# Loading q's and k's second pieces through SP in float32 instead of through GpSimd in bf16

## The chip, the core and the metric

The kernel runs on one core of one Trainium2 chip. The metric is the device time of one execution in microseconds. The times in this document come from repeated runs; the traces come from one profiled execution each, whose own time is given beside them. The engines are called TensorE, VectorE (DVE in the profile), ScalarE (ACT), GpSimd (POOL) and SyncE (SP). A load can be issued from SP, ScalarE or GpSimd; loads issued from GpSimd change float32 to bf16 on the way in this kernel, those from SP and ScalarE copy the bytes as they are.

## What is computed

Sliding-window attention with a linear distance bias over a batch of 8 with 8 heads, 576 positions and a head size of 64, followed by a two-layer block whose nonlinearity is h cos(h):

```python
scores = (q @ k.T) / sqrt(D)                    # per batch and head, float32 inputs
rel = pos[:, None] - pos[None, :]
scores = where((rel >= 0) & (rel < 128), scores - slopes[h] * abs(rel), -1e9)
attn = softmax(scores)
x = (attn @ v).transpose(0, 2, 1, 3).reshape(4608, 512)
h = x @ w_in                                    # 512 -> 2048
out = (h * cos(h)) @ w_out                      # 2048 -> 512, float32 output
```

## The kernel before

The work on TensorE is done in bf16. Attention runs in units: a unit is a batch, a block of 128 queries and (for blocks 1 to 3) half of the heads; a batch has eight units. For a unit, `scores` multiplies keys and queries into two PSUM banks, `exps` takes the exponential on ScalarE, `mask` multiplies by the bias and window factors on VectorE (the first units in `BIASED` instead get the bias added by a matmul on the same banks, in `scores`), `pv` multiplies by V, `norm` divides by the sum, and `x_pe` or `x_dma` transposes the result into `xT`. The two-layer block then takes 512 tokens at a time (`NCH` = 9 chunks): `moe1` makes 128 features of h and its cosine, `moe2` multiplies by W_out and stores. Chunk 0 is cut finer (`moe1_part`), so that it can begin with the first 128 tokens.

Queries and keys must stand with the head size on partitions. For batches 0 and 1 TensorE transposes them (`qk_transposes`), and VectorE or ScalarE copies the transposed bank to `tr`; for later batches DMA transposes do. Batch 0 comes in four pieces of tokens, so that its first unit can start early:

```python
PIECES = {0: [(0, 4, [(0, 4)]), (128, 4, [(0, 4)]), (256, 8, [(0, 4), (4, 8)]), (512, 2, [(0, 2)])], ...
```

Piece 0 covers tokens 0 to 127, piece 1 (the second) 128 to 255, piece 2 (the third) 256 to 511, piece 3 the last 64. Piece 0 is loaded by SP (q) and ScalarE (k) in float32 into `qF` and cast on VectorE or ScalarE to `qC`. The other pieces are loaded by GpSimd straight into bf16 (`qB`, `qE`). GpSimd's loads are issued in the order in which they are written: q's and k's second pieces, V's first block, q's and k's third pieces, V's second block, then W_in, more of V, the last pieces, q and k of batch 1, W_out and V of batch 1.

Every step is given to a planner (`Plan.op`) with what it reads and writes, the engine or the engines that may do it, how long it occupies the engine (`occ`), when its result is there (`lat`), and a priority (`pri`, low first). `Plan.schedule` runs through time with these figures and writes the order of each engine; among what can start at about the same time it takes the lowest priority, then what was created first. `emit` then writes the engines' programs in that order, with waits on semaphores. On the chip each engine follows its order and waits where the figures were wrong. For GpSimd's loads the planner keeps one `wire`:

```python
wire = max(wire, st + 2300) + o.lat              # starts at 4000
o.end = max(wire, st + o.occ + 1400) + 500
```

while a load on SP or ScalarE that is no transpose and no store ends at `st + o.lat`. In the first microseconds TensorE also runs matmuls on zeros (`filler`, line 944) where the plan has nothing else for it.

In the main program, the loads are created first (lines 878 to 893), then the transposes of the first two pieces (lines 895 to 897) and of k's third piece (line 898), which go to PSUM banks 0 and 1. Then `attention(every[0:7], -1)` (line 901) creates the first seven units, two at a time on banks 4, 5 and 6, 7; the transposes of q's third piece are created inside it after the second unit (line 843), on banks 6 and 7.

Of the kernel before, what the change touches and what calls it, by code (L numbers as in the profile page):

```python
# [7 lines left out]
ACTF = mybir.ActivationFunctionType  # L8
F32 = mybir.dt.float32
# [25 lines left out]
class Plan:  # L35
# [16 lines left out]
    def op(self, eng, fn, r=(), w=(), dma=None, occ=100, lat=None, pri=5, mode=0, table=None,  # L52
           after=()):
        o = Op()
        o.seq = len(self.all)
        o.eng = (eng,) if isinstance(eng, str) else tuple(eng)
        o.fn, o.r, o.w, o.dma = fn, tuple(r), tuple(w), dma
        o.occ, o.lat, o.pri, o.mode, o.table = occ, occ if lat is None else lat, pri, mode, table
        preds = {}
        for k in o.r:  # L60
            if k in self.writer:
                preds[self.writer[k]] = DATA
        for k in o.w:
            if k in self.writer:
                preds[self.writer[k]] = DATA
            for d in self.readers.get(k, ()):
                preds.setdefault(d, WAR)
        if dma is not None and dma in self.lastdma:
            preds[self.lastdma[dma]] = DATA
        for d in after:  # L70
            preds.setdefault(d, ORDER)
        if eng == "pool":
            if eng in self.lastseq:
                preds.setdefault(self.lastseq[eng], ORDER)
            self.lastseq[eng] = o
        if dma is not None:
            self.lastdma[dma] = o
        o.preds, o.succs, o.npred = preds, [], len(preds)
        for d in preds:
            d.succs.append(o)  # L80
        for k in o.r:
            self.readers.setdefault(k, []).append(o)
        for k in o.w:
            self.writer[k], self.readers[k] = o, []
        self.all.append(o)
        return o
# [200 lines left out]
def bass_alibi_sliding__then__act_gcu_kernel(  # L287
# [8 lines left out]
    with ExitStack() as ctx:  # L296
        def sb(name, shape, dt=BF16):
            return ctx.enter_context(nc.sbuf_tensor(name, shape, dt))

        R = Plan(nc, ctx)  # L300
        op = R.op
# [3 lines left out]
        xT = sb("xT", [128, NPAIR, NTOK])  # L305
        gT = [sb(f"gT{i}", [128, NFC, CH]) for i in range(2)]
        qF = {"q": sb("qfirst", [128, 2, 256], F32), "k": sb("kfirst", [128, 2, 256], F32)}
        qC = {"q": sb("qcast", [128, 4, 2, 64]), "k": sb("kcast", [128, 4, 2, 64])}
        qB = {"q": sb("qrows", [128, 2, 1152]), "k": sb("krows", [128, 2, 1152])}
        qE = {"q": sb("qend", [128, 2, 128]), "k": sb("kend", [128, 2, 128])}  # L310
# [51 lines left out]
        def piece_keys(which, b, n):  # L362
            return [("qB", which, i) for i in range(3)] if b else [("qB", which, n)]

        def load_qk(which, src, b, n=0):
            t0, rr, _ = PIECES[b][n]
            c0 = 64 * (t0 // 32)
            rows = bass.AP(src.tensor, src[b].offset + 64 * t0,
                           [[64 * rr, 32], [64 * S, H], [1, 64 * rr]])
            if b == 0 and n == 0:  # L370
                op("sp" if which == "q" else "act", [lambda e: e.dma_start(qF[which][:, :, :], rows)],
                   w=[("qF", which)], dma=f"ld{which}f", occ=700 if which == "q" else 2000,
                   lat=4000 if which == "q" else 3300, pri=0)
                i = qF[which][:, :, :].rearrange("p y (j d) -> p y j d", j=4)
                o = qC[which][:, :, :, :].rearrange("p j y d -> p y j d")
                op(("act", "dve"),
                   {"act": lambda e: e.activation(o, i, ACTF.Copy),
                    "dve": lambda e: e.tensor_copy(o, i)},
                   r=[("qF", which)], w=piece_keys(which, b, n), occ={"act": 460, "dve": 330},
                   lat={"act": 560, "dve": 410}, pri=2)  # L380
                return
            o = qE[which][:, :, :] if t0 == 512 else qB[which][:, :, c0:c0 + 64 * rr]
            op("pool", [lambda e: e.dma_start(o, rows)],  # L383
               w=piece_keys(which, b, n), dma=f"ld{which}{n}", occ=750,
               lat={2: 600, 4: 800 if which == 'q' else 900,
                    8: 2600 if which == 'q' else 1300, 18: 2850}[rr])

        def load_v(b, order=range(NBLK), behind=()):
            for t in order:
# [440 lines left out]
        def attention(us, phase):  # L830
# [45 lines left out]
            return begin  # L876

        load_qk("q", q, 0, 0)
        load_qk("k", k, 0, 0)
        constants()  # L880
        load_qk("q", q, 0, 1)
        load_qk("k", k, 0, 1)
        load_v(0, [0])
# [27 lines left out]
        for c in range(NCH):  # L911
# [17 lines left out]
            n = QUOTA[c] if c < len(QUOTA) else 0  # L929
# [46 lines left out]
```

## Time and profile before

| | |
|---|---|
| median of 3 runs | 310.22 us (309.71 to 310.29) |
| the profiled execution | 309.37 us, of which its span is 307.2 us |
| TensorE busy | 298.8 us (97%) |
| VectorE, ScalarE, GpSimd busy | 194.2, 200.0, 97.0 us |
| granted TensorE clock | 1.00 |
| DMA | 39.08 MB, mean 127 GB/s |

A line of the profile gives the engine, the line of the kernel, the operation, the output and the input by the program's names, and their shape. In a timeline a row starts with its start and its duration in us; the bracket at its end gives how long the engine had been idle before it and what released it. "PEld" is TensorE's weight load. A matmul's duration includes its way through the array, so the rows of matmuls that follow one another overlap. In the rows of DMA issues the last number is the time from the issue to the landing. In the windows, each row is a stretch of the span with its length, the busy time of TensorE, its weight loads, VectorE, ScalarE and GpSimd (with the number of instructions), the granted clock, the share of the DMA engines and their GB/s.

### The profile page before, as it was taken

The page shows a single profiled execution, that of the slowest core. Times are in us where ns is not written, and L with a number is a line of the kernel's source. Part 1 is how long each engine was busy: PE and PEld are TensorE (multiplying, and loading weights), DVE is VectorE, ACT ScalarE, POOL GpSimd, SP SyncE. Part 2 cuts the span into 40 slices and gives each one's busy share as a digit, 9 for nine tenths or more (in the row PEclk, how much of TensorE's full clock was granted, in tenths as well). Part 3 has the DMA queues.
Part 4 walks back from the last instruction along what each step waited for, and adds up shares of the span by engine and source line. Part 5 has one row for each costly group of instructions (what it writes and reads, how often), then busy time and mean ns, then how long its engine had stood idle before and what let it go on. Part 6 is the DMA issues. An engine that isn't in the chain of part 4 may idle for free.

```text
span 307.2 us, 6416 instructions
## 1 busy us (share of the span) xinstructions
PE 298.8 (97%) x2556; PEld 156.6 (51%) x2600; DVE 194.2 (63%) x407; ACT 200.0 (65%) x268; POOL 97.0 (32%) x122
## 2 busy tenths in 40 slices
PE   7899999999999999999999999999999999999996
PEld 5585455445544555445544554455445554444444
DVE  7687776674668566856785578657966588742000
ACT  7888855885498646883688378736964588752211
POOL 8997201364055505550357033900500000000000
PEclk9999999999999999999999999999999999999999
DMA  9999999999499939997699969995991420002112
GB/s 142 175 204 207 207 164 191 169 151 181 111 133 144 189 78 144 136 169 103 149 132 150 145 117 148 156 183 114 140 117 44 113 68 2 0 0 70 68 74 97
DMA packets 150332, 39.08 MB, mean 127 GB/s; under 512 B 138912, under 2 KB 145312, under 8 KB 150304
## 3 DMA queue, kind: packets, MB, share of 16 engines
q0 software_dynamic: 100688, 18.10, 79.9%
q1 hardware_dynamic: 49344, 20.33, 32.9%
q8 instruction: 20, 0.33, 0.5%
q10 hardware_dynamic: 272, 0.26, 0.3%
q14 instruction: 8, 0.07, 0.1%
HBM read 36.70 MB, written 9.44 MB: 150 GB/s over the span
## 4 chain that ended last, share of the span: by engine, by line
PE 83%; DMA 7%; POOL 5%; ACT 2%; issue 1%; DVE 1%; POOLq 0%; ACTq 0%
PE ps L812 37%; PE ps L759 36%; DMA w_outb<-in_moe_w_out_dram 7%; PE ps L568 5%; ACT p L595 2%; PE ps L642 2%; PE ps L644 2%; POOL vp L391 1%; PE ps L630 1%; POOL w_inb L423 1%; POOL qrows L383 1%; POOL krows L383 1%; PE ps L634 1%; DVE p L614 1%; POOL w_outb L430 0%
## 5 line engine op out<-in xcount | busy, mean ns | idle before, releaser
L812 PE MATMUL ps<-w_outb,gT 128*128 128x512 bf16 (+2 forms) x566 | 132.8, 373 | 2.3 <-issue 1.1
L759 PE MATMUL ps<-xT,w_inb 128*128 128x512 bf16 x528 | 120.8, 379 | 0.9 <-issue 0.2
L768 DVE TENSOR_TENSOR gT<-ps,cos 128x512 bf16<-128x512 f32 x136 | 90.3, 688 | 21.0 <-ACT cos L764 16.1
L764 ACT ACTIVATE cos<-ps,halfpi 128x512 f32<-128x512 f32 x136 | 90.0, 688 | 18.9 <-PE ps L759 13.9
L595 ACT ACTIVATE p<-ps 128x1024 bf16<-128x1024 f32 x64 | 61.7, 1023 | 32.9 <-PE ps L568 32.8
L759 PEld LDWEIGHTS ps<-xT,w_inb 128*128 128x128 bf16 x544 | 52.0, 98 | 59.5 <-ACT p L595 0.6
L812 PEld LDWEIGHTS ps<-w_outb,gT 128*128 128x128 bf16 x592 | 53.4, 98 | 55.8 <-DMA w_outb<-in_moe_w_out_dram 0.9
L391 POOL DMA_DIRECT2D vp<-in_v_dram x40 | 33.7, 865 | 90.1 <-DMA xT<-xnat 70.2
L614 DVE TENSOR_TENSOR p<-p,emask 128x1024 bf16<-128x1024 bf16 x58 | 39.2, 682 | 26.8 <-ACT p L595 26.7
L819 ACT ACTIVATE ob<-ps 128x512 f32<-128x512 f32 (+2 forms) x21 | 12.1, 576 | 41.8 <-PE ps L812 35.3
L402 POOL DMA_DIRECT2D qnat<-in_q_dram x30 | 25.3, 872 | 21.5 <-DMA qt<-qnat 21.5
L402 POOL DMA_DIRECT2D knat<-in_k_dram x30 | 25.4, 876 | 9.5 <-DMA kt<-knat 7.4
L681 DVE TENSOR_TENSOR xnat<-ps,rec 128x256 bf16<-128x256 f32 x48 | 19.8, 420 | 1.3
L820 DVE COPY ob<-ps 128x512 f32<-128x512 f32 x16 | 10.9, 684 | 15.1 <-PE ps L812 15.1
L568 PE MATMUL ps<-qt,kt 64*128 64x128 bf16 (+1 forms) x576 | 19.4, 211 | 0.4 <-DVE qt L525 0.2
L568 PEld LDWEIGHTS ps<-qt,kt 64*128 64x128 bf16 x576 | 14.5, 94 | 9.7 <-issue 4.5
L642 PEld LDWEIGHTS ps<-vp,p 128*128 128x128 bf16 x192 | 14.2, 97 | 8.8 <-issue 6.1
L644 PE MATMUL ps<-vp,p 128*128 128x65 bf16 x192 | 17.5, 193 | 0.0
L642 PE MATMUL ps<-vp,p 128*128 128x65 bf16 x192 | 17.5, 193 | 0.0
L644 PEld LDWEIGHTS ps<-vp,p 128*128 128x128 bf16 x192 | 13.2, 97 | 2.3
L679 DVE RECIPROCAL rec<-ps 128x4 f32<-128x4 f32 x48 | 8.2, 176 | 6.1 <-PE ps L644 5.6
L630 PEld LDWEIGHTS ps<-vp,p 128*128 128x128 bf16 x128 | 7.3, 97 | 3.6 <-issue 1.8
(66 smaller groups left out, 147.9 us busy)
## 6 DMA issues: line engine op xcount, KB each, us to landing
out_dram<-ob SPq DMA_DIRECT2D x35, 256.0 KB, 2.2
vp<-in_v_dram POOLq DMA_DIRECT2D x32, 128.0 KB, 7.4
qnat<-in_q_dram POOLq DMA_DIRECT2D x24, 128.0 KB, 6.6
knat<-in_k_dram POOLq DMA_DIRECT2D x24, 128.0 KB, 5.2
w_outb<-in_moe_w_out_dram POOLq DMA_DIRECT2D x4, 512.0 KB, 21.2
w_inb<-in_moe_w_in_dram POOLq DMA_DIRECT2D x3, 512.0 KB, 11.7
qrows<-in_q_dram POOLq DMA_DIRECT2D x1, 576.0 KB, 14.8
krows<-in_k_dram POOLq DMA_DIRECT2D x1, 576.0 KB, 16.9
```

The costliest lines, as they stand in the source:

```text
L391: op("pool", [lambda e, t=t, rows=rows: e.dma_start(vp[b % 2][0:rows, t, :, 0:64], v[b, :, 128 * t:128 * t + rows, :].rearrange("h p d -> ...
L402: fns.append(lambda e, t=t, rows=rows: e.dma_start(nat[which][0:rows, t, :, :], src[b, :, 128 * t:128 * t + rows, :].rearrange("h p d -> p ...
L568: ins = e.matmul(ps[:, banks[x], c0:c0 + n_], keys_ap(b, x, pr, kc), query_ap(b, x, pr, qb, n_), start=not acc, stop=stop)
L595: op("act", lambda e: e.activation(P[i][:, 0:1024], ps[:, banks[0]:banks[0] + 2, :].rearrange("p a b -> p (a b)"), ACTF.Exp, scale=0.125), ...
L614: op("dve", lambda e: e.tensor_tensor(p, p, m, ALU.mult), r=[("P", i), ("EM", 0), ("EM", 1)], w=[("P", i)], occ=600, lat=690, pri=1)
L642: e.matmul(o, P[i][:, c0:c0 + 128], V[:, qb - 1, h, 0:65], start=True, stop=False)
L644: ins = e.matmul(o, P[i][:, c0 + 128:c0 + 256], V[:, qb, h, 0:65], start=False, stop=True)
L681: op("dve", lambda e: e.tensor_tensor(o, U[:, :, :, 0:64], rv[:, :, :, None].broadcast_to([128, 2, 2, 64]), ALU.mult), r=[("rec", n % 4)], ...
L759: op("pe", lambda e, kc=kc: e.matmul(ps[:, bank, :], w_in[:, kc, 128 * fc:128 * fc + 128], xT[:, kc, r0:r0 + CH], start=(kc == 0), stop=(k ...
L764: op("act", lambda e: e.activation(cosb[ci][:, :], ps[:, bank, :], ACTF.Sin, bias=halfpi[:, 0:1]), r=["halfpi"], w=[("B", bank), ("cos", c ...
L768: op("dve", lambda e: e.tensor_tensor(gT[gi][:, fc, :], ps[:, bank, :], cosb[ci][:, :], ALU.mult), r=[("cos", ci)], w=[("B", bank)] + [("g ...
L812: op("pe", lambda e, t=t, fc=fc, bank=bank, j0=j0, j1=j1: e.matmul(ps[:, bank, 0:j1 - j0], gT[gi][:, fc, 128 * t:128 * t + 128], w_out[:, ...
```

## The change

Q's and k's second pieces of batch 0 are issued by SP in float32 into two new buffers, and each gets a cast on VectorE or ScalarE into the place where GpSimd's load put it. GpSimd's list of loads then begins with V's first block. The planner gets figures for the two new steps, and its figure for q's third piece on the wire goes from 2600 to 2000; the figure for pieces of 4 rows is used by no load any more.

```diff
@@ -305,6 +305,7 @@
         qF = {"q": sb("qfirst", [128, 2, 256], F32), "k": sb("kfirst", [128, 2, 256], F32)}
+        qS = {"q": sb("qsecond", [128, 2, 256], F32), "k": sb("ksecond", [128, 2, 256], F32)}
         qC = {"q": sb("qcast", [128, 4, 2, 64]), "k": sb("kcast", [128, 4, 2, 64])}
@@ -380,10 +381,20 @@
             o = qE[which][:, :, :] if t0 == 512 else qB[which][:, :, c0:c0 + 64 * rr]
+            if b == 0 and n == 1:
+                i = qS[which][:, :, :]
+                op("sp", [lambda e: e.dma_start(i, rows)], w=[("qS", which)], dma=f"ld{which}s",
+                   occ=700, lat=3900, pri=0)
+                op(("act", "dve"),
+                   {"act": lambda e: e.activation(o, i, ACTF.Copy),
+                    "dve": lambda e: e.tensor_copy(o, i)},
+                   r=[("qS", which)], w=piece_keys(which, b, n), occ={"act": 460, "dve": 330},
+                   lat={"act": 560, "dve": 410}, pri=2)
+                return
             op("pool", [lambda e: e.dma_start(o, rows)],
                w=piece_keys(which, b, n), dma=f"ld{which}{n}", occ=750,
-               lat={2: 600, 4: 800 if which == 'q' else 900,
-                    8: 2600 if which == 'q' else 1300, 18: 2850}[rr])
+               lat={2: 600, 4: 1300,
+                    8: 2000 if which == 'q' else 1300, 18: 2850}[rr])
```

## The prediction

> **What bounds the kernel now.** I read the page's busy shares and its chain first, then the windows of the first 16 us, then the timeline of the head and the DMA landings.
>
> ```profile
> PE 298.8 (97%) x2556; PEld 156.6 (51%) x2600; DVE 194.2 (63%) x407; ACT 200.0 (65%) x268; POOL 97.0 (32%) x122
> PE 83%; DMA 7%; POOL 5%; ACT 2%; issue 1%; DVE 1%; POOLq 0%; ACTq 0%
> PE ps L812 37%; PE ps L759 36%; DMA w_outb<-in_moe_w_out_dram 7%; PE ps L568 5%; ACT p L595 2%; PE ps L642 2%; PE ps L644 2%; POOL vp L391 1%; PE ps L630 1%; POOL w_inb L423 1%; POOL qrows L383 1%; POOL krows L383 1%; PE ps L634 1%; DVE p L614 1%; POOL w_outb L430 0%
> ```
>
> TensorE is busy for 298.8 of 307.2 us, and the chain is TensorE for 83%. The 7% of DMA and 5% of GpSimd on it are the loads that start the kernel, up to W_out. So the time is TensorE's work plus what it stands still, and the standstill lies in the head. The windows show where:
>
> ```profile
> 8.00:10.00 2.00, 1.56 (x27) 0.90 (x30) 0.71 (x3) 1.60 (x3) 2.00 (x3) 1.00 1.37 169
> 10.00:12.00 2.00, 1.69 (x37) 1.22 (x37) 1.32 (x4) 1.86 (x4) 2.00 (x4) 1.00 1.70 173
> 12.00:14.00 2.00, 1.85 (x31) 1.33 (x32) 1.78 (x6) 1.16 (x2) 2.00 (x4) 1.00 2.19 165
> 14.00:16.00 2.00, 2.00 (x42) 1.37 (x40) 0.97 (x4) 1.62 (x3) 2.00 (x4) 1.00 1.40 204
> ```
>
> From 8 to 14 us TensorE is idle 0.44, 0.31 and 0.15 us in three windows of 2 us, and from 14 us on not at all. The busy figure is generous to pipelined matmuls, so the true slack there is somewhat larger. An edit in the head that leaves later stages alone is worth what it does to these gaps. The head's order in the trace:
>
> ```profile
> 6.60 0.41 PE L509 MATMUL ps<-ident,krows 128*64 128x128 bf16 x8 [0.28 <-DMA krows<-in_k_dram]
> 7.61 1.97 ACT L595 ACTIVATE p<-ps 128x1024 bf16<-128x1024 f32 x2
> 8.78 0.40 PE L630 MATMUL ps<-vp,p 128*128 128x65 bf16 x8 [0.26 <-ACT p L595]
> 9.23 0.38 PE L582 MATMUL ps<-bias,ident 128*128 128x512 bf16 x1
> 9.54 0.40 PE L568 MATMUL ps<-qt,kt 64*128 64x128 bf16 x8
> 9.95 0.48 PEld L509 LDWEIGHTS ps<-ident,qrows 128*64 128x64 bf16 x16 [0.18 <-DMA qrows<-in_q_dram]
> 9.95 0.64 PE L509 MATMUL ps<-ident,qrows 128*64 128x128 bf16 x16
> 10.63 0.69 DVE L525 COPY qt<-ps 128x512 bf16<-128x512 bf16 x1 [0.29 <-PE ps L509]
> 11.23 0.64 PE L509 MATMUL ps<-ident,krows 128*64 128x128 bf16 x16 [0.32 <-DMA krows<-in_k_dram]
> 11.91 0.69 DVE L525 COPY kt<-ps 128x512 bf16<-128x512 bf16 x1 [0.40 <-PE ps L509]
> 12.91 0.40 PE L568 MATMUL ps<-qt,kt 64*128 64x128 bf16 x8
> 13.35 2.12 ACT L595 ACTIVATE p<-ps 128x1024 bf16<-128x1024 f32 x2 [0.84 <-PE ps L568]
> ```
>
> Call the seven units of batch 0 that run in this stage u0 to u6. The row at 6.60 is the transposes of k's second piece; the first exponentials are u0 and u1 (7.61, 0.99 us each); 8.78 is the P times V of u0; 9.23 and 9.54 are the bias and the scores of u2; 9.95 the transposes of q's third piece; 11.23 those of k's third piece; 12.91 the scores of u3, the first unit that needs both third pieces. ScalarE stands still 0.84 us before the exponential of u3 at 13.35. This is the wait that ends last in the head, and it goes back to the landing of k's third piece.
>
> **What is moved between the queues.** The loads concerned and the time from each issue to its landing:
>
> ```profile
> 0.74 0.75 SPq L371 DMA_DIRECT2D qfirst<-in_q_dram  x1
> 0.75 0.71 ACTq L371 DMA_DIRECT2D kfirst<-in_k_dram  x1
> 1.36 0.85 POOL L383 DMA_DIRECT2D qrows<-in_q_dram  x1 [0.18 <-issue]
> 2.20 0.72 POOL L383 DMA_DIRECT2D krows<-in_k_dram  x1
> 2.92 0.94 POOL L391 DMA_DIRECT2D vp<-in_v_dram  x1
> 3.85 0.70 POOL L383 DMA_DIRECT2D qrows<-in_q_dram  x1
> 4.54 0.72 POOL L383 DMA_DIRECT2D krows<-in_k_dram  x1
> ```
>
> ```profile
> qfirst<-in_q_dram SPq DMA_DIRECT2D x1, 256.0 KB, 4.1
> kfirst<-in_k_dram ACTq DMA_DIRECT2D x1, 256.0 KB, 3.3
> qrows<-in_q_dram POOLq DMA_DIRECT2D x1, 128.0 KB, 4.0
> krows<-in_k_dram POOLq DMA_DIRECT2D x1, 128.0 KB, 4.4
> vp<-in_v_dram POOLq DMA_DIRECT2D x1, 128.0 KB, 4.5
> qrows<-in_q_dram POOLq DMA_DIRECT2D x1, 256.0 KB, 6.1
> krows<-in_k_dram POOLq DMA_DIRECT2D x1, 256.0 KB, 6.6
> ```
>
> Adding: the second pieces land at 1.36 + 4.0 = 5.4 (q) and 2.20 + 4.4 = 6.6 (k), V's first block at 2.92 + 4.5 = 7.4, the third pieces at 3.85 + 6.1 = 9.95 and 4.54 + 6.6 = 11.1. The change removes two issues from GpSimd, 0.85 + 0.72 = 1.57 us, so every later issue comes about that much sooner. That alone is worth little: the third pieces already wait 6 us behind their issue, so what counts is how fast the bytes go. The rate in steps of 0.1 us from 2 to 6 us:
>
> ```profile
> GB/s 0 0 61 92 92 82 20 20 225 266 358 348 358 379 369 389 379 379 389 399 338 282 251 220 195 200 195 180 143 149 184 143 138 143 149 146 140 128 157 145
> ```
>
> From 3.0 to 4.0 us the two float32 pieces run at 348 to 399, near 375 GB/s: 262 KB / 375 = 0.70 us for one. From 4.8 us the second pieces and V run in bf16 at 128 to 184, mostly near 145 GB/s: 131 KB / 145 = 0.90 us for one; at the 195 to 200 of 4.4 to 4.6 us it would be 0.67 us. So the two pieces leave GpSimd's queue 2 x 0.90 us lighter and load SP's with 2 x 0.70 us. If both queues share one capacity, which the falling sums from 4.0 to 4.7 us suggest (338 down to 180 as the float32 pieces run out), the stream behind gains 1.80 - 1.40 = 0.4 us; by the faster bf16 figure it loses 0.06; if the float32 bytes cost nothing beside the others, it gains 1.8. I take 0.3 us, near the first, since the 145 GB/s rows lie just where these pieces move. K's third piece then lands at 10.8 and not at 11.1.
>
> [...]
>
> **The second pieces themselves.** SP issued q's first piece from 0.74 for 0.75 us, so the new issues start at 1.49 and 2.24. At the 4.1 us of that piece they land at 5.6 and 6.3; nothing else is queued on SP in the head, so nothing waits behind them there. Then come the casts, which before do not exist for these pieces; the rows of the first pieces are the same shape:
>
> ```profile
> 4.55 0.41 DVE L378 CAST kcast<-kfirst 128x512 bf16<-128x512 f32 x1
> 5.01 0.47 DVE L378 CAST qcast<-qfirst 128x512 bf16<-128x512 f32 x1
> 7.06 0.60 ACT L524 ACTIVATE kt<-ps 128x512 bf16<-128x512 bf16 x1 [0.49 <-PE ps L509]
> ```
>
> A cast is 0.41 to 0.47 us. K's is done at 6.3 + 0.45 = 6.8, and its transposes start near 6.85 in place of 6.60: 0.25 us late. ScalarE is idle 0.49 us just before 7.06, so the casts have room, and q's falls ahead of that. A cast waits in its engine's order for the landing; behind it stand the copies of the first and second transposes and the exponential of u0. So u0 and u1 move 0.25 us later, u0's P times V to about 9.0. If they wait longer (rival B) this cover is gone.
>
> **The order, which moves too.** The program's planner writes a fixed order for TensorE from due times that it adds up from `occ` and `lat`. I use them for the order only. Before, they gave k's third piece 4.0 + 0.8 + 0.9 + 0.896 + 2.6 + 1.3 + 0.5 = 11.0, close to the 11.1 above. After, q's and k's second pieces no longer count on that wire and q's third piece is set to 2.0: 4.0 + 0.896 + 2.0 + 1.3 + 0.5 = 8.7. That is 2.3 us sooner in the plan, where the bytes give 0.3. The float32 bytes on SP's queue are in no term. So the transposes of k's third piece, planned at 8.75 to 9, are put ahead of u2's bias and scores: they have the same priority 2 and are created earlier (line 898 against 901), and u2's banks 4 and 5 come free only when the exponential of u0 ends, 7.61 + 0.99 = 8.6. Before, they stood behind u2 and q's third piece.
>
> TensorE issues in order. After u0's P times V it would reach these transposes at about 9.2 and stand until 10.85, 1.65 us, with u2's bias and scores and q's transposes queued behind. Then: transposes 0.48 us (the weight loads' row at 9.95), u2's bias 2 x 0.22 and scores 0.23, as they follow each other at their pitch (estimates from the 9.23 and 9.54 rows, whose 0.38 and 0.40 hold the tail), so q's transposes start at 10.85 + 0.48 + 0.44 + 0.23 = 12.0. From there to their copies is 10.63 - 9.95 = 0.68, a copy 0.69, and from the copies' end to u3's scores as before 12.91 - 11.91 - 0.69 = 0.31: 12.0 + 1.68 = 13.7. Before it was 12.91, so u3 is 0.8 us late. If q's transposes come ahead of u2 they start at 11.35 and u3's scores at 13.0, 0.1 late; if the exponential of u2 keeps ScalarE from its copy and VectorE has both, another 0.69 late, 1.5. I take 0.8: u2's banks are free before q's target banks 6 and 7, which the exponential of u1 holds until about 9.6 in the trace and 0.25 later after.
>
> **The sum.** The units u3 to u6 follow one another and TensorE is full from 14 us, so 0.8 us at u3 is taken as 0.8 us of TensorE standing still. One thing gives some back:
>
> ```profile
> 38.77 1.04 PE L812 MATMUL ps<-w_outb,gT 128*128 128x512 bf16 x4 [0.19 <-DMA w_outb<-in_moe_w_out_dram]
> PE ps L812 <- DMA w_outb<-in_moe_w_out_dram: 0.2, 1, 0.2
> PEld ps L812 <- DMA w_outb<-in_moe_w_out_dram: 0.9, 2, 0.7
> ```
>
> At 38.77 TensorE waits for W_out, 0.19 us by its own row and 0.9 by its weight loads' in two places. TensorE arriving 0.8 later and W_out 0.3 sooner removes this: -0.2 (up to -0.9). Sum: +0.8 - 0.2 = +0.6; with u0 and u1 late by 0.25 in part (they lie ahead of the stall, and I count 0.1), +0.7 us. The profiled execution took 309.37 us, of which the span is 307.2 and 2.2 lie around it; it would be 310.1. The median of the runs is 310.22, 0.85 above that execution, so I predict 310.9. The two casts, 0.9 us of VectorE or ScalarE, are otherwise hidden: neither bounds TensorE in the head outside the chain above.
>
> **Rivals.**
> A, faster: the float32 bytes run beside GpSimd's stream and cost it nothing, so the third pieces, V, W_in and W_out come up to 1.8 us sooner. Then k's third piece lands at 9.4, the stall is 0.2 us, q's transposes start at 10.55 and u3's scores at 12.2, 0.7 us sooner; the W_out wait goes too, 0.2: -0.9, 309.3. The 399 GB/s peak speaks for spare capacity, the 145 GB/s just behind for a stream that was not fed; the falling sums speak against.
>
> B, slower: SP's second pieces are served in turns with GpSimd's and land late. At half of 375 GB/s each takes 1.4 us, from 4.84 (q's first landing, 0.74 + 4.1) to 6.2 and 7.6; k's transposes start at 8.1 and not 6.6, 1.5 us late, and u0's scores stand behind them. The stall for the third piece covers part of it, about 0.8 us; +0.7 more gives 311.6. It decides when k lands after about 7. For it: kfirst landed 0.8 us ahead of qfirst with issues 0.01 apart. [...]
>
> C, no change: q's transposes come before u2, or the early W_in fills what opens; the 0.1 late and the 0.2 of W_out cancel: 310.1.
>
> That the change does nothing (same order) is not possible, since the due times differ; C stands for it.
>
> **How the numbers follow.** A measurement of this kernel tells about 0.2%, 0.62 us, from no change. Forecast 0.45 (310.9, its own range 310.5 to 311.8; a fourth of it inside 0.62 us), B 0.14, C 0.15, A 0.26. Faster 0.25 (A nearly whole), slower 0.34 + 0.14 = 0.48, same 0.11 + 0.15 + 0.01 = 0.27. The range reaches from A's 309.3 to the forecast's upper bound (1.5 at u3) and past B, 311.9.
>
> **What would show it.** Right: the transposes of k's third piece in the PE rows ahead of u2's scores with 1 to 2 us of idle before them, released by the krows DMA; krows landing near 10.8; u3's exponential near 14.1; two casts near 5.7 to 6.8; no W_out wait near 38. Wrong: krows landing below 10, u2's scores ahead of those transposes, or u3's exponential before 13.35.

## The result, and the profile after

| | before | after |
|---|---|---|
| median | 310.25 us (309.71 to 310.75, 6 runs) | 313.13 us (311.96 to 314.03, 6 runs) |
| ratio, with its 95% interval | | 1.0099 [1.0082, 1.0116] |
| the profiled execution | 309.37 us | 311.96 us |
| last exponential of the head ends | 17.72 us | 20.34 us |

The changed kernel is slower by 1%, 2.9 us between the medians and 2.6 us between the two profiled executions. The head loses all of this: the last row of the table is the end of the seventh exponential of batch 0's first stage (u6), 15.78 + 1.94 before and 17.28 + 3.06 after. The row of before is this one; that of after is the last one of the timeline further down (in the changed kernel line numbers are up to 11 higher):

```profile
15.78 1.94 ACT L595 ACTIVATE p<-ps 128x1024 bf16<-128x1024 f32 x2 [0.31 <-PE ps L568]
```

The page of after, with its busy shares, the granted clock in 40 slices (7.75 us each) and the engines of the chain:

```profile
PE 301.1 (97%) x2559; PEld 158.4 (51%) x2603; DVE 196.0 (63%) x409; ACT 200.7 (65%) x268; POOL 95.5 (31%) x120
...
PEclk9799999999999999999999999999999999999999
...
PE 87%; DMA 5%; ACT 3%; DVE 2%; issue 1%; SPq 1%; ACTq 0%
```

Two things differ from before. The second slice of the clock is 7, where the kernel before had its full clock; and DMA is 5% of the chain in place of 7%, since W_out's load is no longer on it. The timeline of the head, with both queues' issues:

```profile
1.53 0.84 SPq L386 DMA_DIRECT2D qsecond<-in_q_dram  x1
1.83 1.02 POOL L402 DMA_DIRECT2D vp<-in_v_dram  x1 [0.65 <-DVE vp L465]
2.42 0.61 SPq L386 DMA_DIRECT2D ksecond<-in_k_dram  x1
2.84 0.70 POOL L394 DMA_DIRECT2D qrows<-in_q_dram  x1
3.54 0.71 POOL L394 DMA_DIRECT2D krows<-in_k_dram  x1
6.14 0.89 DVE L390 CAST qrows<-qsecond 128x512 bf16<-128x512 f32 x1 [0.63 <-DMA qsecond<-in_q_dram]
8.79 0.63 ACT L389 ACTIVATE krows<-ksecond 128x512 bf16<-128x512 f32 x1 [2.53 <-DMA ksecond<-in_k_dram]
9.47 0.41 PE L520 MATMUL ps<-ident,krows 128*64 128x128 bf16 x8 [1.37 <-ACT krows L389]
9.82 0.40 PE L579 MATMUL ps<-qt,kt 64*128 64x128 bf16 x8
10.26 2.18 ACT L606 ACTIVATE p<-ps 128x1024 bf16<-128x1024 f32 x2 [0.35 <-PE ps L579]
11.95 1.06 PE L520 MATMUL ps<-ident,krows 128*64 128x128 bf16 x16
12.81 1.06 PE L520 MATMUL ps<-ident,qrows 128*64 128x128 bf16 x16
14.40 0.40 PE L579 MATMUL ps<-qt,kt 64*128 64x128 bf16 x8
14.84 2.11 ACT L606 ACTIVATE p<-ps 128x1024 bf16<-128x1024 f32 x2 [0.33 <-PE ps L579]
15.49 0.40 PE L579 MATMUL ps<-qt,kt 64*128 64x128 bf16 x8
17.28 3.06 ACT L606 ACTIVATE p<-ps 128x1024 bf16<-128x1024 f32 x3 [0.33 <-PE ps L579]
```

The landings of the two queues, from issue to landing in the last column:

```profile
qsecond<-in_q_dram SPq DMA_DIRECT2D x1, 256.0 KB, 4.6
ksecond<-in_k_dram SPq DMA_DIRECT2D x1, 256.0 KB, 6.3
qrows<-in_q_dram POOLq DMA_DIRECT2D x1, 256.0 KB, 7.2
krows<-in_k_dram POOLq DMA_DIRECT2D x1, 256.0 KB, 7.8
```

K's second piece lands at 2.42 + 6.3 = 8.7. Its cast, its transposes (9.47, before 6.60), the scores of u0 (9.82) and u0's exponential (10.26, before 7.61) follow each other with no slack: u0 is 2.65 us late. Then come the transposes of k's third piece (11.95) and of q's (12.81), and only then the scores of u2 (14.40, before 9.54) and of u3 (15.49, before 12.91). K's third piece lands at 3.54 + 7.8 = 11.3, against 11.1 before: GpSimd's stream, now lighter by two loads, gained nothing. The same matmuls also take longer. The 16 transposes are 1.06 us in place of 0.64, and the windows show why (columns as in the prediction; the eighth entry, after POOL, is the granted clock):

```profile
7.10:10.50 3.40, 1.46 (x30) 1.01 (x29) 1.39 (x4) 1.36 (x3) 3.40 (x6) 1.00 1.48 192
10.50:13.90 3.40, 3.16 (x50) 2.62 (x50) 1.59 (x5) 2.40 (x3) 1.45 (x2) 0.51 1.97 174
13.90:17.30 3.40, 3.21 (x51) 1.77 (x53) 2.23 (x8) 2.66 (x4) 2.85 (x5) 0.99 1.34 205
```

After 3.4 us in which TensorE was busy 1.46 us, it was granted half its clock for 3.4 us, just while the transposes of both third pieces ran. This execution is a mild one: its mean clock is 0.994, that of one other of the six runs 0.995 and that of four 0.989, and since 3.4 us at half the clock take about 0.0055 off the mean of 310 us, those four lost about twice as much (an estimate). The run at 0.995 took 313.92 us, so the clock alone doesn't order the times.

### The profile page after: what moved, and what is told of

The parts are those of the page before. It is cut to its first block, busy times and chain, and to the rows that moved or that the text cites. A ratio compares the mean times of both kernels' runs of the same rounds, so it can differ in the third digit from the quotient of the medians.

```text
span 310.1 us, 6422 instructions
## 1 busy us (share of the span) xinstructions
PE 301.1 (97%) x2559; PEld 158.4 (51%) x2603; DVE 196.0 (63%) x409; ACT 200.7 (65%) x268; POOL 95.5 (31%) x120
## 4 chain that ended last, share of the span: by engine, by line
PE 87%; DMA 5%; ACT 3%; DVE 2%; issue 1%; SPq 1%; ACTq 0%
PE ps L770 37%; PE ps L823 35%; PE ps L579 5%; DMA xT<-xfirst 3%; ACT p L606 3%; PE ps L794 2%; DMA ksecond<-in_k_dram 2%; PE ps L653 2%; PE ps L520 2%; PE ps L641 1%; PE ps L655 1%; DVE p L625 1%; PE ps L645 1%; PE ps L732 0%; PE ps L593 0%
```

## The experiments

Three causes were open: the late landing of k's second piece, the order that the planner wrote, and the halved clock. The first question was whether one of them alone makes the whole loss. In the table, "head ends" is the end of the seventh exponential in the one profiled execution, whose own time stands beside it; the ratio is to the kernel before on the same chip.

| label | what it is | ratio [95%] | profiled, us | head ends, us |
|---|---|---|---|---|
| e1_due | after, planner told the true landings | 1.0093 [1.0058, 1.0128] | 310.92 | 19.90 |
| e2_warm | after, zeros in the gap | 1.0119 [1.0102, 1.0137] | 313.65 | 21.16 |
| e3_alone | after, GpSimd starts when k has landed | 1.0109 [1.0092, 1.0126] | 313.56 | 22.68 |
| e4_konly | before, only k's second piece on SP | 0.9974 [0.9959, 0.9989] | 308.42 | 17.96 |
| e8_late | before, k's second piece late, same order | 1.0122 [1.0096, 1.0149] | 313.8 | 22.58 |
| e9_latewarm | e8_late with zeros in the gap | 1.007 [1.0045, 1.0094] | 312.63 | 21.14 |
| e5_vlate | after, V's first block behind the third pieces | 1.011 [1.0069, 1.0151] | 314.37 | 23.71 |
| e7_act | after, k's second piece on ScalarE's queue, 0.94 us sooner | 1.0095 [1.007, 1.0119] | 312.11 | 20.16 |
| e10_act_due | e7_act, planner told the true landings | 0.9999 [0.9985, 1.0012] | 310.77 | 19.01 |
| e6_oldfig | after, old figure for q's third piece | 1.0119 [1.0103, 1.0136] | 312.93 | 21.28 |
| e11_konly2 | e4_konly again | 0.9983 [0.9969, 0.9997] | 309.7 | 18.21 |
| e12_actwarm | e7_act with zeros in the gap | 1.0101 [1.0067, 1.0134] | 312.1 | 19.79 |

**e1_due: the order mended, the loads as in after.**

```diff
-        wire = 4000
+        wire = 7500
...
-                   occ=700, lat=3900, pri=0)
+                   occ=700, lat=4600 if which == "q" else 6600, pri=0)
...
-                    8: 2000 if which == 'q' else 1300, 18: 2850}[rr])
+                    8: 1130 if which == 'q' else 1300, 18: 2850}[rr])
```

> The changed kernel with the planner's figures set to what the changed kernel's trace shows (SP's second pieces 4.6 us for q, and landing at 8.75 for k; GpSimd's wire from 7.5, so that V's first block is due at 8.9, q's and k's third pieces at 10.0 and 11.3). The loads are the same, only the orders differ: u0's scores now stand ahead of the transposes of k's second piece. If late landing is the cause (theory): k's second piece still lands near 8.8, u1 and u3 wait for it, and 1.0 to 1.5 us of the loss stay, near 311.5. If the order written from wrong due times is the cause (rival): the loss goes, 310.3 to 310.8.

Measured: 312.44 us (310.9 to 314.7, 7 runs). Rows of its timeline:

```profile
7.52 0.40 PE L579 MATMUL ps<-qt,kt 64*128 64x128 bf16 x8
...
9.82 0.41 PE L520 MATMUL ps<-ident,krows 128*64 128x128 bf16 x8
...
11.23 0.62 PE L579 MATMUL ps<-qt,kt 64*128 64x128 bf16 x16
11.78 0.64 PE L520 MATMUL ps<-ident,krows 128*64 128x128 bf16 x16
```

U0's scores now run ahead of the late transposes, and two units' scores ahead of those of k's third piece. Still most of the loss stays: units that need k's second piece wait for it, whatever the order. In this execution the clock was full, so the halved clock isn't needed for a loss either. The runs of this kernel lie wide apart, and the interval allows anything from half of the loss to more than all of it.

**e2_warm: 24 matmuls of zeros on TensorE between q's and k's second transposes of after**, to keep it busy in the gap.

> The changed kernel with 24 more matmuls on zeros between the transposes of q's and of k's second piece, so that TensorE does not stand idle while it waits for k. All else is in the same order. If the half clock from 10.5 to 13.95 us is a part of the loss of its own (theory): the clock stays at 1.0 in the windows, the third pieces' transposes take 0.64 us again in place of 1.06, and the time is 1.0 to 1.3 us under the changed kernel's, near 311.9. If the clock only stretches what has room (rival): no gain beyond 0.3 us.

Measured: 313.58 us, no gain. Its profiled execution had the full clock, but k's piece came later than in after, with the same loads in the same order:

```profile
10.53 0.63 ACT L389 ACTIVATE krows<-ksecond 128x512 bf16<-128x512 f32 x1 [4.28 <-DMA ksecond<-in_k_dram]
```

So this says little on the clock: the cast of k's piece started 1.7 us later than in after (8.79) with the same loads, and its other three runs had a mean clock of 0.995, about one stretch of 3.4 us at half the clock each by the estimate above.

**e3_alone: V's first load, and with it all of GpSimd's, waits until k's second piece has landed.**

```diff
-                   r=[("vinit", b % 2)] + [x.w[0] for x in behind], w=[("v", b % 2, t)],
+                   r=[("vinit", b % 2)] + [x.w[0] for x in behind] +
+                   ([("qS", "k")] if b == 0 and t == 0 else []), w=[("v", b % 2, t)],
```

> The changed kernel, but GpSimd's first load (V's first block) waits until k's second piece has landed, so that SP's float32 pieces have the DMA engines to themselves. If GpSimd's packets hold SP's up (theory): q lands at 4.1 to 4.6 us after its issue and k at 4 to 4.5 after its own, near 6.5 to 6.9, in place of 6.3 after. If SP's queue is slow by itself (rival): k still lands 6 us or more after its issue. The time says less, since GpSimd's whole stream starts some 4.7 us later: 312 to 315.

Measured: 313.26 us. The landings, and where TensorE stands instead:

```profile
qsecond<-in_q_dram SPq DMA_DIRECT2D x1, 256.0 KB, 4.8
ksecond<-in_k_dram SPq DMA_DIRECT2D x1, 256.0 KB, 4.5
```

```profile
15.18 0.64 PE L521 MATMUL ps<-ident,krows 128*64 128x128 bf16 x16 [1.62 <-DMA krows<-in_k_dram]
```

Without GpSimd's packets beside it k's piece lands 4.5 us after its issue, at 6.9, where after took 6.3 us and e2_warm 8.1. The packets show the same. In the profile's list of DMA queues q0 is GpSimd's, q1 SP's and q10 ScalarE's, each with its packets, MB and share of the DMA engines. From 5.0 to 5.5 us after has

```profile
q0 software_dynamic: 314, 0.04, 124.9%
q1 hardware_dynamic: 53, 0.05, 33.8%
```

and e3_alone moves 0.16 MB on SP's queue in the same half microsecond, with nothing of GpSimd's. GpSimd's stream holds SP's second piece up. The time is no better because the third pieces now start late.

**e4_konly and e11_konly2: before, with only k's second piece moved to SP**, q's left in GpSimd's queue, and its time told to the planner as 4.6 us.

> The kernel before with only k's second piece on SP in float32 with a cast; q's second piece stays first on GpSimd's queue, all planner figures of GpSimd's loads as before. If sharing with GpSimd's packets is what makes a piece late (theory): k has one piece less ahead of it on SP and lands 4.6 to 5.2 us after its issue at 1.5, near 6.4, its transposes start near 7.0, and the time is within 0.5 us of before, 309.8 to 310.7. If anything second on SP lands late (rival): k lands past 7.5 and the time is 1 us or more above before.

> The kernel of e4_konly again (k's second piece alone on SP, all of GpSimd's figures as before), on one chip with the other two and in five rounds, to settle whether it beats before. By e4_konly: 0.997 of before, 308.6 to 309.4 where before is 309.9. If that was a better landing by chance: 0.999 to 1.002.

Measured: a small gain in both, 0.9974 and 0.9983. The landings, first of e4_konly, then of e11_konly2:

```profile
ksecond<-in_k_dram SPq DMA_DIRECT2D x1, 256.0 KB, 4.7
krows<-in_k_dram POOLq DMA_DIRECT2D x1, 256.0 KB, 6.5
```

```profile
ksecond<-in_k_dram SPq DMA_DIRECT2D x1, 256.0 KB, 4.8
krows<-in_k_dram POOLq DMA_DIRECT2D x1, 256.0 KB, 7.5
```

A single float32 piece on SP, issued at 1.54, lands in time (6.2 and 6.3), so it is the second one, issued 0.9 us later, that runs into GpSimd's stream. Whether the stream gains is not steady: k's third piece, issued at 3.78, lands at 10.3 in one execution and at 11.3 in the other. The head of both ends 0.2 to 0.5 us later than before's, so where this gain comes from isn't shown; e4's profiled execution, the fastest of ten, has no wait for W_out, and e11's still has 0.6 us of it.

**e8_late and e9_latewarm: the late landing and the gap, without the change.** In before, k's second piece is put behind q's third in GpSimd's queue, with its due time in the plan held where it was, so that the order stays. The second kernel adds 24 matmuls of zeros in the gap.

```diff
+                    if o.dma == "ldk1":
+                        o.end = 6200
...
-        load_qk("k", k, 0, 1)
...
+        load_qk("k", k, 0, 1)
```

> The kernel before with no float32 piece, no cast and no SP load: only k's second piece moved behind q's third piece in GpSimd's queue, and its due time in the planner pinned to 6.2 us, so that all other engines keep the order of before. Its landing should move from 6.6 to about 9.3. If the in-order stall behind that landing is the whole loss (theory): the transposes of k's second piece start near 9.4, everything behind is 2.0 to 2.8 us late, 311.9 to 312.7. If the loss needs the second queue's traffic, the casts or the other order (rival): under 1 us, 310.0 to 310.8.

> The run e8_late with 24 matmuls on zeros ahead of the transposes of k's second piece, which TensorE runs while it would stand. The landing is the same, so the difference to e8_late is the clock's: if the half clock window after the stall costs (theory): the clock is 1.0 in all windows and the time 0.5 to 1.2 us under e8_late. If it falls on work that has room (rival): within 0.3 us of e8_late.

Measured: 313.74 us (312.38 to 313.9) and 311.72 us (311.2 to 312.63). K's second transposes, in e8_late and in e9_latewarm:

```profile
10.28 0.64 PE L511 MATMUL ps<-ident,krows 128*64 128x128 bf16 x8 [4.01 <-DMA krows<-in_k_dram]
```

```profile
9.94 0.41 PE L511 MATMUL ps<-ident,krows 128*64 128x128 bf16 x8 [2.11 <-DMA krows<-in_k_dram]
```

The same transposes take 0.64 us at half clock and 0.41 at the full one, which e9_latewarm kept in all four runs. Between the medians lie 2.0 us, of which 0.34 may be the earlier landing in the second profile: in this kernel some 1.7 of the 4.3 us lost are the clock, by this estimate, and the rest is the late landing. In after's profile the clock's part may be smaller: e8_late's clock was halved from 8.8 to 15.6 us, twice as long. Its one run with a mean clock of 0.994 took 312.38 us, the three with 0.989 took 313.69 to 313.9.

**e5_vlate: V's first block behind the third pieces in GpSimd's queue**, so that SP's pieces meet the larger packets of q and k there: up to 6.5 us GpSimd's queue moves 0.28 MB in 293 packets, near 960 bytes each, where after's moves 0.11 MB in 784, near 140 bytes each.

```diff
-        load_v(0, [0])
...
+        load_v(0, [0])
```

> The changed kernel with V's first block moved behind the third pieces in GpSimd's queue, so that SP's float32 pieces meet packets of 1024 bytes in place of V's of 128 bytes. If V's many small packets hold SP's pieces up (theory): k's second piece lands near 6.8, as in e3_alone, or up to 7.5. If any full stream of GpSimd does (rival): k's second piece lands at 8.5 or later as in the changed kernel. The time mixes this with V's later landing and another order of TensorE: 310.5 to 313.

Measured: 313.22 us (311.45 to 314.37). Q's piece landed at 8.8 and k's at 10.9, later still. That the packets of V are the special hindrance falls; beside a stream that begins with q's and k's third pieces k's piece took 8.5 us to land, against 6.3 in after.

**e6_oldfig: after with q's third piece planned at 2600 as before.**

> The changed kernel with the planner's old figure of 2600 for q's third piece in place of 2000, nothing else. Its due times become 0.6 us later, still 1.5 to 2 us ahead of the landings, and k's second piece still lands late. If the missing float32 traffic in the plan is what matters and not this figure (theory): within 0.7 us of the changed kernel's 313.1. If the figure by itself spoils the order (rival): 311.5 or less.

Measured: 313.47 us. The changed figure isn't needed for the wrong order: the transposes of k's third piece still stand ahead of u2's scores (13.71 and 15.27). The time says nothing on it, since k's second piece landed at 9.6 here, and a late landing keeps the loss whatever the order (e1_due). What else moved the plan is, by the code, that two pieces no longer count on its wire; that part wasn't undone alone.

**e7_act: after, with k's second piece issued by ScalarE behind k's first.** This changes its queue, and with it the time of its issue, 1.48 in place of 2.42.

```diff
-                op("sp", [lambda e: e.dma_start(i, rows)], w=[("qS", which)], dma=f"ld{which}s",
+                op("sp" if which == "q" else "act", [lambda e: e.dma_start(i, rows)], w=[("qS", which)], dma=f"ld{which}s",
```

> The changed kernel with k's second piece issued by ScalarE right after its first piece, so that it has a queue of its own and is issued near 1.5 in place of 2.4. If each queue gets its turns (theory): the two float32 pieces together have two turns of three, and k's second piece lands 1 to 2 us earlier than 8.8, at 6.8 to 7.8, with 311 to 312. If the bytes have to share what is left beside GpSimd's stream (rival): it lands at 8.3 or later and the time stays at 312.5 to 313.5.

Measured: 312.3 us (312.11 to 313.16). Landings, timeline, one window, and the queues from 4.0 to 5.0 us:

```profile
ksecond<-in_k_dram ACTq DMA_DIRECT2D x1, 256.0 KB, 4.2
qsecond<-in_q_dram SPq DMA_DIRECT2D x1, 256.0 KB, 4.9
```

```profile
7.70 0.41 PE L520 MATMUL ps<-ident,krows 128*64 128x128 bf16 x8
...
10.85 0.64 PE L520 MATMUL ps<-ident,krows 128*64 128x128 bf16 x16 [1.46 <-DMA krows<-in_k_dram]
...
12.21 1.06 PE L520 MATMUL ps<-ident,qrows 128*64 128x128 bf16 x16
13.21 0.61 PE L579 MATMUL ps<-qt,kt 64*128 64x128 bf16 x8
...
15.15 0.56 PE L579 MATMUL ps<-qt,kt 64*128 64x128 bf16 x8
```

```profile
12.10:15.50 3.40, 3.40 (x39) 2.07 (x38) 2.26 (x7) 1.59 (x3) 1.65 (x3) 0.50 1.70 191
```

```profile
q10 hardware_dynamic: 265, 0.26, 73.2%
q1 hardware_dynamic: 137, 0.12, 36.0%
```

K's second piece lands at 1.48 + 4.2 = 5.7, sooner than the 6.8 to 7.8 expected, and its transposes stand at 7.70. It wasn't beside GpSimd's stream: its 0.26 MB were moved from 4.0 to 5.0, and GpSimd's queue has no packet before 5.0. So the run doesn't say whether the queue of its own or the sooner issue got it through; in e4_konly and e11_konly2, with q's piece left to GpSimd, the sooner issue was enough on SP's queue. The run is the nearest to the prediction's case: the transposes of k's third piece are put ahead of u2, and TensorE stands there 1.46 us (1.65 predicted) until 10.85 (10.85 predicted). That the last two agree so well is luck, since with the same loads the wait ended at 11.55 in e12_actwarm below. The loss is 0.95%, as large as in after: the wrong order is enough by itself.

**e10_act_due: e7_act, with the planner told the true landings**, so that loads and order are both mended.

```diff
-        wire = 4000
+        wire = 6200
...
-                   occ=700, lat=3900, pri=0)
+                   occ=700, lat=4900 if which == "q" else 4300, pri=0)
...
-                    8: 2000 if which == 'q' else 1300, 18: 2850}[rr])
+                    8: 1950 if which == 'q' else 1300, 18: 2850}[rr])
```

> The run e7_act (k's second piece on ScalarE's queue, landing near 5.7) with the planner's figures set to the landings of that run: GpSimd's wire from 6.2 and q's third piece 1.95, so that V's first block is due at 7.6 and q's and k's third pieces at 9.55 and 10.85; q's second piece 4.9, k's 4.3. If late landing and wrong due times are each enough for the loss, and together all of it (theory): with both mended the stall ahead of k's third transposes and the half clock go, and the time is 309.0 to 310.3, within 0.3% of before. If the float32 pieces cost something else, in DMA or in the casts (rival): 311 or more.

Measured: 309.96 us, 0.9999 [0.9985, 1.0012], with the full clock. K's second piece took 5.2 us to land, at 6.7, and q's 5.4. The scores of u2 and the transposes of k's third piece:

```profile
10.69 0.40 PE L579 MATMUL ps<-qt,kt 64*128 64x128 bf16 x8
11.38 0.64 PE L520 MATMUL ps<-ident,krows 128*64 128x128 bf16 x16 [0.29 <-DMA krows<-in_k_dram]
```

U2 is ahead of the third piece again, and the loss is gone. What differs from e7_act is figures of the plan alone, so this shows the order's part in e7_act; and with e1_due, which has the same kind of figures but keeps k behind q on SP and lands it at 8.9, it shows the landing's part. (The profiled execution is the slowest of its runs with one other, 0.8 us above their median.)

**e12_actwarm: e7_act with 24 matmuls of zeros ahead of the third piece's transposes.**

> The kernel of e7_act with 24 more matmuls of zeros (128x512, bf16, into a bank that the real outputs overwrite later) on TensorE directly ahead of the transposes of k's third piece, where e7_act's TensorE stood 1.46 us for that piece's rows (9.4 to 10.85) and was then granted half its clock from about 12 to 15. The order, the loads and all outputs stay. Theory (the loss of e7_act is in part the halved clock after the gap): granted clock 1.0 from 12 to 15, and the time 0.8 to 1.5 us below e7_act's 312.3, near 311.0. Rival (the order alone costs all of it, the halved clock falls on time in which ScalarE is late anyway): clock 1.0, but the time within 0.3 us of 312.3. Should the landing of k's third piece come early enough, the zeros themselves may delay its transposes by up to 1 us, which would hide a gain; the profile's start of these transposes (10.85 in e7_act) tells.

Measured: 312.68 us (311.94 to 313.7), no gain. The timeline and the window:

```profile
11.55 0.64 PE L520 MATMUL ps<-ident,krows 128*64 128x128 bf16 x16 [0.75 <-DMA krows<-in_k_dram]
...
12.90 0.64 PE L520 MATMUL ps<-ident,qrows 128*64 128x128 bf16 x16
13.47 0.40 PE L579 MATMUL ps<-qt,kt 64*128 64x128 bf16 x8
...
14.94 0.40 PE L579 MATMUL ps<-qt,kt 64*128 64x128 bf16 x8
```

```profile
12.10:15.50 3.40, 3.20 (x59) 1.93 (x57) 2.65 (x7) 2.23 (x4) 1.39 (x2) 1.00 1.79 185
```

The clock is full, and the stretch from the third piece's transposes to u3's scores is shorter, 14.94 - 11.55 = 3.39 us where e7_act took 15.15 - 10.85 = 4.30. That is some 0.9 us for the clock in this stretch. But k's third piece landed 0.7 us later in this execution, the zeros were over by then, and the time shows nothing. So the theory holds for the stretch and not for the time; what the halved clock costs after's median is not settled.

## Why the prediction was right or wrong

The side was right, and so was one of the two mechanisms behind it, the order. Wrong were the landing of k's second piece and the price of the order, and with them the size: +2.9 us where +0.7 was forecast, outside the range.

**The step that failed first: "they land at 5.6 and 6.3".** Q's second piece landed at 6.13, k's at 8.7. The prediction took the 4.1 us of q's first piece, of which 0.20 of 0.26 MB had moved by 4.0 us with only k's first piece beside it, for a piece that is issued 1.7 us later and meets GpSimd's stream. Rival B named the mechanism, sharing with that stream, and sized it at 7.6. The runs bear out the sharing, and B too was short. From its issue to its landing k's second piece took

- 4.5 us on SP without GpSimd's stream (e3_alone),
- 4.1 to 5.2 us when it was issued 0.9 us sooner on ScalarE's queue (e7_act, e10_act_due, e12_actwarm),
- 4.7 and 4.8 us when it was issued as early on SP's (e4_konly, e11_konly2),
- 6.3 to 8.5 us on SP behind q's piece and beside the stream (after, e1_due, e2_warm, e6_oldfig, e5_vlate).

E3_alone against after, 4.5 us against 6.3, shows that the stream holds this piece up. That the queues are served in turns, as rival B had it, no run here shows.

**"The stream behind gains 0.3 us": not in after.** GpSimd's issues came 1.0 us sooner and not 1.57 (k's third at 3.54, before 4.54), because V's first load now stood first and waited 0.65 us for V's memset. All of that was lost on the way: 7.8 us to land where it had been 6.6. K's third piece landed at 11.3 there, and at 10.8 in e7_act and 11.5 in e12_actwarm with the same loads: a term of 0.3 us is smaller than this spread. At 11.1, no gain, the prediction's sum would come to 310.9 + 0.3 = 311.2, still 1.9 us short, so this term was not the one that mattered. With k's piece alone moved it landed at 10.3 (e4_konly) and 11.3 (e11_konly2), against 11.1 before, so whether the stream gains is not settled by these runs.

**The order: right in its main part.** The transposes of k's third piece stand ahead of u2's scores, as worked out from the due times. But q's transposes, which the prediction put behind u2's scores, stand ahead of them too (12.81 and 14.40 in after, 12.21 and 13.21 in e7_act). It had priced that case at u3's scores at 13.0. The stall forecast ahead of k's third piece, 1.65 us, isn't in after, because TensorE arrived only at 11.95, after its landing; it stands 1.37 us at k's second transposes instead. In e7_act it is there at its place and almost at its size, and TensorE kept its written order: q's third piece had landed at 2.84 + 6.7 = 9.5 and its banks came free at 8.48 + 1.97 = 10.45, and still its transposes ran behind k's, at 12.21.

**"0.8 us at u3": too small, even in e7_act.** There u3's scores come at 15.15, 2.2 us later than before's 12.91, and were forecast for 13.7. At the full clock the way from these transposes to u3's scores took 3.39 us (e12_actwarm), where the sum had 13.7 - 10.85 = 2.85: P times V of u0 came behind the third piece and not ahead of it, and transposes of u0's output with two biases came between u2's and u3's scores. The halved clock adds some 0.9 us. The prediction carried the clock of 1.00 from before over to a kernel whose TensorE it expected to stand for 1.65 us.

**Forecast and rival B were treated as alternatives.** They have one origin and came together, and their prices do not add: the late landing alone keeps the loss (e1_due, 1.0093), the order alone too (e7_act, 1.0095), both together cost 1.0099, and with both mended it is 0.9999. In the traces either one sends u3 to about the same late place: its scores come at 15.49 in after, at 15.15 in e1_due and in e7_act, and at 14.30 with both mended. Why the two end up in the same place, through different orders, isn't shown. With 0.14 for B the chances said that most likely k lands in time; the row that spoke for B, two equal loads issued 0.01 us apart and landing 0.8 apart, should have weighed more than that.

**Smaller terms.** W_out is off the chain, as forecast, with 0.3 us of waits left in its weight loads. The casts take 0.89 and 0.63 us where 0.45 was forecast, and k's is on the chain, also as forecast. Rival A, free capacity, falls: k's third piece did not come before 10.3 in any of these kernels. Rival C's time, no change, is where the change ends when its plan is right and k is issued early on ScalarE's queue.

## What to carry to other kernels

A load moved to a queue that is empty is not a load served alone: ask whether its bytes will be through before the stream that it leaves begins, price it beside that stream if not, and take the landing of a load without the stream only as the lower bound (here 4.5 us without it, 6.3 to 8.5 as the second piece on SP beside it). Where a planner's due times decide the order, changing what it counts is an edit of the order too, and a wrong due time can cost more than the bytes gain: the plan's figures alone were worth 0.95% here (e7_act against e10_act_due). Losses in one head that push the same unit late need not add (here 0.93% and 0.95% alone, 0.99% together), so mending one may show nothing; test them both apart and together.

## What the runs showed of the hardware

TensorE's clock was halved although TensorE had not been idle for the 3.4 us before: in after it was busy 1.46 of 3.40 us from 7.10 to 10.50, and the granted clock was 0.51 from 10.50 to 13.90, a drop of about 3.4 us. E9_latewarm kept a clock of 1.00 with 1.35 of 3.40 us busy from 8.00 to 11.40. So the busy share of such a stretch doesn't tell by itself whether the clock falls; what does, no run here shows. Landings of the same loads differ between executions by 1.0 us (k's third piece in e4_konly and e11_konly2) to 1.7 us (k's second piece in after and e2_warm, by the start of its cast), more than most of the terms of the prediction.
